# One decode step of an attention block: another order of the first loads, ScalarE sums 16 rows of query 0, one SBUF tensor for keys and values, other pieces for the last values

## The chip, the core and the metric

The kernel runs on one core of a Trainium2 chip. The metric is the device time of one launch in microseconds, the median of several runs. The engines that matter are VectorE (DVE), TensorE (PE), ScalarE (ACT), and the queue of SyncE (SP), which issues all but one of the loads. The loads run on 16 DMA engines.

## What is computed

A transformer block for one new token in each of two sequences: attention over a cache of 8192 positions with 16 heads of 256, and then a bilinear gated feed-forward layer. All is float32.

```
h  = x + (softmax(q k^T / 16) v) wo     q = layernorm(x) wq, B=2, H=16, Sk=8192, Dh=256, D=448
h2 = h + ((n wg) * (n wu)) wd           n = layernorm(h), F=1792
```

Each of the 32 pairs of head and sequence (called a query here, numbers 0 to 31) reads its own 8 MB of keys and 8 MB of values. With the weights that is 561 MB in all.

## The kernel before

A query's keys and values stand as 128 partitions of 64 rows of 256 numbers; a load of all 64 rows is 8192 KB. The scores are made on DVE: one TENSOR_TENSOR multiplies rows by the query's vector in place, one TENSOR_REDUCE sums each row. The product with the values is made on TensorE: for two rows at a time a matmul of 2 columns of `p` against 2x256 values, which the chip runs as two instructions, so that 64 rows are 64 rows of MATMUL in the trace.

Keys stand in a ring of 112 rows (`k_sb`). Even queries start at row 0 and odd ones at row 48, so that rows 48 to 63 are shared by neighbours. `score_parts` begins each query with those 16 shared rows: when the first product and sum are done, the shared rows are free and `load_k(n + 1)` can be issued. Values stand in `v_sb`, 64 rows; `load_v` of a query waits until TensorE has read the values of the query before.

Program order is set by the loop over `n` at the end of `decode_block`: load the values of query `n-1`, first scores of query `n` (with the softmax of query `n-1` between product and sum), load the keys of query `n+1`, further pieces of the values, the rest of the scores, the product with the values (`mix`), the maximum (`top`). SP takes its loads strictly in that order and waits in it; the DMA engines work off what SP has issued in order. Waits are worked out by a recorder (`Orders`) from the regions that each operation reads and writes.

The last queries are written apart: `LATE` gives the pieces in which their values are loaded and where, `FINE` makes queries 30 and 31 score 16 rows at a time, so that places come free earlier. Behind the last values come the feed-forward weights: gate (`wg`, one load), up (`wu`, two), down (`wd`, four). `open_sums` puts the sum so far (`h_sb`) into PSUM, `mixed` transposes the attention output, `project` is the gate or up product, `down` the down product. All lines of the trace read L229 or L176, since one helper writes all instructions and one issues all loads.

At the start the first weights (`d_w0`, 896 KB) are loaded, then query 0's keys in two pieces: rows 40 to 63, then rows 0 to 39. The product of the first piece goes into `v_sb`. TensorE makes the two heads' query vectors for both sequences before the loop.

Of the kernel before, what the change touches and what calls it, by code (L numbers as in the profile page):

```python
# [6 lines left out]
AF = mybir.ActivationFunctionType  # L7
# [11 lines left out]
OVER = HC  # L19

AHEAD = 24
FIRST = ((NJ - AHEAD, NJ), (0, NJ - AHEAD))


LATE = (
    ((48, None), (16, None)),
    ((32, None), (32, None)),
    ((32, None), (32, ("k", 0))),
    ((16, ("k", 32)), (32, ("v", 32)), (16, ("v", 0))),
)  # L30
WQ, WO = 3 * 2 * DH + DH, 2 * D
WALL = 2 * WQ + 4 * WO
# [183 lines left out]
def decode_block(nc, x, k_cache, v_cache, w, wg, wu, wd, out):  # L216
# [25 lines left out]
        put("PE", "transpose", out, in_, ident[:n, :n], r=(*r, "ident"), w=w, mark=mark)  # L242

    sb("align", P, ALIGN)
    k_sb = sb("k_sb", P, 2 * NJ - OVER, DH)
    v_sb = sb("v_sb", P, NJ, DH)
    w_sb = sb("w_sb", P, WALL)
    buffers = {"k": k_sb, "v": v_sb}
    v_flat = v_sb.rearrange("p j d -> p (j d)")

    def guest(name, at, rows, *shape):

        n = 1
        for k in shape:
            n *= k
        o.homes[name] = ("v", at, n)
        got = v_flat[:rows, at : at + n]
        if len(shape) > 1:
            dims = "abc"[: len(shape)]
            got = got.rearrange(f"p ({' '.join(dims)}) -> p {' '.join(dims)}", **dict(zip(dims, shape)))  # L260
        return got
# [5 lines left out]
        h, b = divmod(i, B)  # L267
        return cache[b, h].rearrange("(p j) d -> p j d", p=P)[:, lo:hi, :]

    def load_keys(name, cache, i, lo, hi, buf, at, event=None):  # L270
        o.load(
            "SP", name, buffers[buf][:, at : at + hi - lo, :], keys(cache, i, lo, hi),
            writes=[(buf, at * DH, (at + hi - lo) * DH)], event=event,
        )

    def k_base(i):
        return i % 2 * (NJ - OVER)

    def load_k(i, lo=0, hi=NJ):
        load_keys(f"d_k_{i}_{lo}", k_cache, i, lo, hi, "k", k_base(i) + lo)  # L280

    def v_parts(i):
        got, lo = [], 0
        for n, place in LATE[i - EARLY] if i >= EARLY else ((NJ, None),):
            buf, at = place or ("v", lo)
            got.append((lo, lo + n, buf, at))
            lo += n
        return got

    def load_v(i, part):  # L290
        lo, hi, buf, at = part
        load_keys(f"d_v_{i}_{lo}", v_cache, i, lo, hi, buf, at, "e_v" if i < LOOP else None)

    def load_w(name, k, lo, hi, event=None):
        o.load("SP", name, w_sb[:, lo:hi], w[k][:, lo:hi], writes=[("w", lo, hi)], event=event)
# [4 lines left out]
    def wo_at(h):  # L300
        return 2 * WQ + h % 4 * WO

    load_w("d_w0", 0, 0, WQ)
    for lo, hi in FIRST:
        load_k(0, lo, hi)

    ident = sb("ident", P, P)
    put("POOL", "memset", ident, 0.0, w=["ident"])
# [77 lines left out]
    def q_at(h):  # L386
        return h % 2 * (1 + h // 2 % 2)

    for k in range(2):
        for b in range(B):  # L390
            for c in range(DC):
                at = c * 2 * DH + (k * DH if c < DC - 1 else 0)
                mm(
                    q_ps[b][:, :DH], xb[:, c + (k if c == DC - 1 else 0), b, :],
                    w_sb[:, at : at + DH], c == 0, c == DC - 1, r=["xb", ("w", 0, WQ)],
                    w=[f"q_ps{b}"], mark="PE" if c == DC - 1 else None,
                )
# [6 lines left out]
    o.settle("PE", ["DVE", "POOL", "ACT"])
    mm(
        acc_ps, ident[:B, :B], x_sb[:, :D], True, False, r=["ident", "x_sb"], w=["acc_ps"],
        mark="PE",
    )
# [34 lines left out]
    def score_parts(i):  # L443
        if i == 0:
            return list(FIRST)
        at = [(k - 1) % (NJ // HC) * HC if i % 2 == 0 else k * HC for k in range(NJ // HC)]
        if i in FINE:
            return [(lo, lo + HC) for lo in at]
        return [(at[0], at[0] + HC), (at[1], at[1] + NJ - HC)]

    def scores(i, part, between=None):
        h, b = divmod(i, B)
        s, name = s_t[i % 2], f"s{i % 2}"
        lo, hi = score_parts(i)[part]
        at = k_base(i) + lo
        kt = k_sb[:, at : at + hi - lo, :]
        qk, there = kt, ("k", at * DH, (at + hi - lo) * DH)
        if i == 0 and part == 0:
            qk, there = v_sb[:, : hi - lo, :], ("v", 0, (hi - lo) * DH)
        q, slot = qs[b], q_at(h)  # L460
        here = ("k", at * DH, (at + hi - lo) * DH)
        dve(
            "tensor_mul", qk, kt, q[:, slot, :][:, None, :].to_broadcast([P, hi - lo, DH]),
            r=[here, (f"q{b}", slot, slot + 1)], w=[there],
        )
        if between is not None:
            between()
        dve("tensor_reduce", s[:, lo:hi], qk, axis=AX.X, op=ALU.add, r=[there], w=[(name, lo, hi)])

    def top(i):  # L470
        dve("tensor_reduce", m, s_t[i % 2], axis=AX.X, op=ALU.max, r=[f"s{i % 2}"], w=["m"],
# [24 lines left out]
    def mix(i, parts):  # L496
        k = other(i)
        with common(i):
            take("e_v", i, 16)
            for lo, hi, buf, at in parts:  # L500
                for t in range(lo // 2, hi // 2):
                    g, j = 32 * (t % 4), at + 2 * t - lo
                    mm(
                        o_ps[k][g : g + 2, :], p_t[k][:, 2 * t : 2 * t + 2],
                        buffers[buf][:, j : j + 2, :], t < 4, t >= NJ // 2 - 4,
                        r=[f"p{k}", (buf, j * DH, (j + 2) * DH)], w=[f"o_ps{k}"],
                        mark="PE" if t == hi // 2 - 1 else None,
                    )

# [71 lines left out]
    def group(t, q):  # L581
        return t[:, q * YW : (q + 1) * YW]

    late_at = [HC * DH]

    def late_guest(name, rows, *shape):
        got = guest(name, late_at[0], rows, *shape)
        late_at[0] += o.homes[name][2]
        assert late_at[0] <= 2 * HC * DH
        return got  # L590

    h_sb = late_guest("h_sb", B, DC * P)
# [19 lines left out]
    for n in range(NQ + 1):  # L612
        hp, at = divmod(n, 2 * B)
        parts = v_parts(n - 1) if n > 0 else []
        if n > 0:
            load_v(n - 1, parts[0])
        if n < NQ:
            scores(n, 0, (lambda: softmax(n - 1)) if n > 0 else None)
        else:
            softmax(n - 1)  # L620
        if late is not None:
            mix(n - 2, late)
            mixed(n - 2)
# [12 lines left out]
        if n == NQ:
            norm_last()
        else:
            for part in range(1, len(score_parts(n))):
                scores(n, part, norm_last if part == 1 else None)  # L640
        if n == NQ:
            mix(n - 1, parts[:-1])
            open_sums()
            mix(n - 1, parts[-1:])
            mixed(n - 1)
        elif n + 1 < NQ and len(parts) > 1:
            late = parts[1:]
            mix(n - 1, parts[:1])
        elif n > 0:
            mix(n - 1, parts)  # L650
            mixed(n - 1)
        if at == 2 and hp + 1 < H // 2:
            queries(n - 1, hp + 1)
        if n < NQ:
            if n == 0:
                o.ops["PE"].append(lambda: turns())
            top(n)

    k_flat = k_sb.rearrange("p j d -> p (j d)")
    places = {"wd": 0, "wg": (NJ - OVER) * DH, "wu": (NJ - OVER) * DH + NF * D}  # L660
    wd_t, wg_t, wu_t = (k_flat[:, places[n] :][:, : NF * D] for n in ("wd", "wg", "wu"))
    for name, t, src in (("wg", wg_t, wg), ("wu", wu_t, wu)):
        for k, half in enumerate(PIECES[name]):
            o.load("SP", f"d_{name}_{k}", t[:, half], src[:, half],
                   writes=[("k", places[name] + half.start, places[name] + half.stop)])
    at = 0
    for n in DOWN:
        o.load("SP", f"d_wd_{at}", wd_t[:, at * D : (at + n) * D], wd[:, at * D : (at + n) * D],
               writes=[("k", at * D, (at + n) * D)])
        at += n  # L670

    o.load(
# [6 lines left out]

    def project(out, out_name, t, name, k, between=None):  # L680
        wide, piece = WIDE[{"wg": "B_w_gate", "wu": "B_w_up"}[name]][k], PIECES[name][k]
        here = ("k", places[name] + piece.start, places[name] + piece.stop)
        t = t[:, piece]
        for c in range(DC):
            for g in range(4):
# [172 lines left out]
```

## Time and profile before

| | |
|---|---|
| time, median of 3 runs | 1301.44 us (1301.37 to 1301.44) |
| span of the profiled execution, first to last instruction | 1300.46 us (1300.5 on the page) |
| time less span: what lies around the span, as the profile has no time of its own | 0.98 us |
| DVE busy | 1130.8 us (87%) |
| PE busy (matmuls) | 488.8 us (38%) |
| ACT busy | 62.6 us (5%) |
| moved by DMA | 561.45 MB, mean 432 GB/s |
| mean granted TensorE clock, share of full speed | 0.654 |

Busy time of an engine counts only instructions that compute. The span is cut into 40 slices on the page, and each digit is the busy share in tenths. The granted clock of TensorE takes two levels, 0.5 and 1.0 of full speed.

### The profile page before, as it was taken

How to read it: one execution, taken by the hardware profiler on the slowest of the kernel's cores; microseconds unless marked ns; L12 is line 12 of the kernel's file. 1: busy time of each engine (PE TensorE's matmuls, PEld its weight loads, DVE VectorE, ACT ScalarE, POOL GpSimd, SP SyncE). 2: the span in 40 equal slices, each digit the busy share in tenths (PEclk: the TensorE clock that was granted, in tenths of full speed). 3: DMA queues.
4: the chain of work that ended last, by engine and by line, in shares of the span. 5: the costliest groups of instructions: out<-in, count | busy, mean ns of one | idle time of the engine just before them, and what ended most of it. 6: DMA issues, size and time to landing. Idle time of an engine off the chain costs nothing.

```text
span 1300.5 us, 6955 instructions
## 1 busy us (share of the span) xinstructions
PE 488.8 (38%) x2972; PEld 168.9 (13%) x2972; DVE 1130.8 (87%) x275; ACT 62.6 (5%) x184; POOL 1.4 (0%) x9
## 2 busy tenths in 40 slices
PE   3035422363331633215343063432424334243368
PEld 2011100120100201002101021010111001010113
DVE  7996988888988689888889868898888897889991
ACT  1000000000000000000000000000000000000000
POOL 0000000000000000000000000000000000000000
PEclk8566756686656766558666576665766667666578
DMA  9999999999999999999999999999999999999998
GB/s 414 423 434 448 424 437 431 427 441 423 448 424 435 448 423 443 427 439 429 435 435 423 433 448 423 448 424 443 427 443 427 423 436 445 426 438 429 435 433 374
DMA packets 12111, 561.45 MB, mean 432 GB/s; under 512 B 1602, under 2 KB 1732, under 8 KB 1988
## 3 DMA queue, kind: packets, MB, share of 16 engines
q1 hardware_dynamic: 12096, 561.30, 99.8%
q8 instruction: 6, 0.10, 0.0%
q14 instruction: 5, 0.04, 0.0%
q10 hardware_dynamic: 4, 0.00, 0.0%
HBM read 561.19 MB, written 0.11 MB: 432 GB/s over the span
## 4 chain that ended last, share of the span: by engine, by line
DMA 70%; DVE 29%; PE 0%; issue 0%; SPq 0%
DMA k_sb<-in_A_k_cache_dram 68%; DVE k_sb L229 14%; DVE s L229 14%; DMA k_sb<-in_wd_dram 2%; DVE nm L229 0%; PE y_ps L229 0%; SPq L176 0%; DVE m L229 0%; PE sm L229 0%; DVE v_sb L229 0%; DVE rl L229 0%
## 5 line engine op out<-in xcount | busy, mean ns | idle before, releaser
L229 DVE TENSOR_TENSOR k_sb<-k_sb,q 128x12288 f32<-128x12288 f32 (+2 forms) x67 | 549.6, 8203 | 130.3 <-DMA k_sb<-in_A_k_cache_dram 130.3
L229 DVE TENSOR_REDUCE s<-k_sb 128x48 f32<-128x12288 f32 (+2 forms) x67 | 549.3, 8198 | 0.2
L229 PE MATMUL o_ps<-v_sb,p 128*2 128x512 f32 x2000 | 288.2, 739 | 397.7 <-PEq L183 387.6
L229 PEld LDWEIGHTS o_ps<-v_sb,p 128*2 128x2 f32 x2000 | 53.7, 97 | 603.8 <-issue 591.3
L229 PE MATMUL sm<-nm,ones 1*128 1x1 f32 x64 | 16.6, 326 | 191.7 <-PEq L183 175.1
L229 PE MATMUL sm<-ident,m 128*1 128x128 f32 x32 | 10.9, 341 | 137.0 <-PEq L183 106.1
L229 PE MATMUL q_ps<-w_sb,xb 128*128 128x256 f32 (+1 forms) x172 | 59.3, 503 | 0.0
L229 ACT ACTIVATE o_sb<-o_ps 128x512 f32<-128x512 f32 x32 | 19.1, 597 | 703.9 <-PE o_ps L229 703.9
L229 PE MATMUL sm<-sel,o_sb 128*128 128x1 f32 x256 | 33.7, 253 | 25.8 <-PEq L183 22.9
L229 PE MATMUL acc_ps<-w_sb,oT 128*2 128x448 f32 x60 | 36.6, 749 | 15.9 <-PEq L183 11.0
L229 PEld LDWEIGHTS sm<-nm,ones 1*128 1x128 f32 x64 | 14.6, 283 | 201.2 <-issue 183.5
L229 PEld LDWEIGHTS sm<-sel,o_sb 128*128 128x128 f32 x256 | 31.8, 195 | 55.6 <-issue 48.2
L229 PEld LDWEIGHTS q_ps<-w_sb,xb 128*128 128x128 f32 x172 | 33.7, 200 | 30.0 <-issue 27.6
L229 PE MATMUL sm<-lsum,ones 128*128 128x1 f32 x64 | 17.5, 342 | 26.0 <-PEq L183 23.1
L229 ACT ACTIVATE nb<-sm 128x1 f32<-128x1 f32 x32 | 5.5, 171 | 395.7 <-PE sm L229 395.7
L229 PEld LDWEIGHTS sm<-ident,m 128*1 128x1 f32 x32 | 2.6, 81 | 149.8 <-issue 115.3
L229 PEld LDWEIGHTS sm<-lsum,ones 128*128 128x128 f32 x64 | 15.6, 303 | 28.0 <-issue 24.7
L229 ACT ACTIVATE q<-q_ps,rstd 128x512 f32<-128x512 f32 (+1 forms) x18 | 11.5, 640 | 71.9 <-PE q_ps L229 71.9
L229 PE MATMUL o_ps<-k_sb,p 128*2 128x512 f32 x48 | 9.3, 934 | 6.1 <-DMA k_sb<-in_A_v_cache_dram 6.1
L229 ACT ACTIVATE p<-s,nb 128x64 f32<-128x64 f32 x32 | 11.1, 347 | 1.0
L229 DVE TENSOR_TENSOR v_sb<-k_sb,q 128x6144 f32<-128x6144 f32 x1 | 6.6, 6557 | 4.8 <-DMA k_sb<-in_A_k_cache_dram 4.8
L229 PE MATMUL q_ps<-k_sb,xr 128*32 128x256 f32 (+3 forms) x96 | 10.0, 506 | 1.6 <-DMA k_sb<-in_B_w_gate_dram 1.6
(79 smaller groups left out, 85.1 us busy)
## 6 DMA issues: line engine op xcount, KB each, us to landing
v_sb<-in_A_v_cache_dram SPq DMA_DIRECT2D x4, 4096.0 KB, 30.5
w_sb<-in_w_dram SPq DMA_DIRECT2D x3, 3584.0 KB, 37.8
v_sb<-in_A_v_cache_dram SPq DMA_DIRECT2D x1, 6144.0 KB, 24.3
k_sb<-in_A_k_cache_dram SPq DMA_DIRECT2D x1, 5120.0 KB, 24.6
v_sb<-in_A_v_cache_dram SPq DMA_DIRECT2D x2, 2048.0 KB, 27.3
k_sb<-in_A_v_cache_dram SPq DMA_DIRECT2D x1, 4096.0 KB, 35.3
k_sb<-in_B_w_gate_dram SPq DMA_DIRECT2D x1, 3136.0 KB, 32.4
k_sb<-in_A_k_cache_dram SPq DMA_DIRECT2D x1, 3072.0 KB, 11.6
```

Source lines behind the costliest of these rows:

```text
L229: o.put(engine, lambda: f(*args, **kw), r, w, mark, event)
```

## The change

Six edits, in the order of the program:

1. SP's first load is query 0's keys, rows 0 to 23, into the place of the values; then `d_w0`; then rows 24 to 63 into the ring. Even and odd queries change places in the ring (even ones at 48), so that query 1's keys (rows 0 to 63) overlap nothing of query 0's.
2. Of the 24 rows of query 0's first piece ScalarE sums 16, one ACTIVATE with an accumulator for each row; DVE sums 8. Head 1's query vectors are made behind that in program order, and TensorE's wait for the other engines (`settle`) ahead of its loop moves behind them too.
3. `k_sb` and `v_sb` become one tensor `c_sb` of 176 rows: ring 0 to 111, values from 112.
4. Query 28 is an ordinary query: its values come in one load of 64 rows, and TensorE's loop covers it. Queries 29, 30 and 31 load in pieces of 32 and 32, of 64, of 44 and 20 rows.
5. The product of query 30's first 16 rows goes to rows 160 to 175, so that `load_k(31)` needs only the product and not the sum.
6. At the end `open_sums` stands before all of query 31's `mix`; the feed-forward weights take other places.

```diff
-FIRST = ((NJ - AHEAD, NJ), (0, NJ - AHEAD))
+FIRST = ((0, AHEAD), (AHEAD, NJ))
+RING = 2 * NJ - OVER
 LATE = (
-    ((48, None), (16, None)),
-    ((32, None), (32, None)),
-    ((32, None), (32, ("k", 0))),
-    ((16, ("k", 32)), (32, ("v", 32)), (16, ("v", 0))),
+    ((32, RING), (32, RING + 32)),
+    ((64, NJ),),
+    ((44, RING + HC), (20, NJ)),
 )
...
     def k_base(i):
-        return i % 2 * (NJ - OVER)
+        return (1 - i % 2) * (NJ - OVER)
...
+    load_keys("d_k_first", k_cache, 0, *FIRST[0], RING)
     load_w("d_w0", 0, 0, WQ)
-    for lo, hi in FIRST:
-        load_k(0, lo, hi)
+    load_k(0, *FIRST[1])
...
-        at = [(k - 1) % (NJ // HC) * HC if i % 2 == 0 else k * HC for k in range(NJ // HC)]
+        at = [(k - i % 2) % (NJ // HC) * HC for k in range(NJ // HC)]
...
+        at = RING if i == 0 and part == 0 else k_base(i) + lo
+        to = RING + NJ - HC if i == NQ - 2 and part == 0 else at
...
-        dve("tensor_reduce", s[:, lo:hi], qk, axis=AX.X, op=ALU.add, r=[there], w=[(name, lo, hi)])
+        if i == 0 and part == 0:
+            for j in range(HC):
+                row = ("c", (to + j) * DH, (to + j + 1) * DH)
+                act(t[:, j, :], t[:, j, :], AF.Copy, accum_out=s[:, lo + j : lo + j + 1],
+                    r=[row], w=[row, (name, lo + j, lo + j + 1)])
+            t, there, lo = t[:, HC:, :], ("c", (to + HC) * DH, (to + hi - lo) * DH), lo + HC
+        dve("tensor_reduce", s[:, lo:hi], t, axis=AX.X, op=ALU.add, r=[there], w=[(name, lo, hi)])
...
         if n < NQ:
+            if n == 0:
+                first_queries(0)
+                open_sum()
             scores(n, 0, (lambda: softmax(n - 1)) if n > 0 else None)
+            if n == 0:
+                first_queries(1)
+                o.settle("PE", ["DVE", "POOL", "ACT"])
...
         if n == NQ:
-            mix(n - 1, parts[:-1])
             open_sums()
-            mix(n - 1, parts[-1:])
+            mix(n - 1, parts)
             mixed(n - 1)
...
-    places = {"wd": 0, "wg": (NJ - OVER) * DH, "wu": (NJ - OVER) * DH + NF * D}
+    places = {"wg": 0, "wu": NF * D, "wd": (NJ + 20) * DH}
```

How SP's queue begins before the change (a row is a load, its shape in numbers per partition, and the engines that it waits for; 6144 numbers are 24 rows of keys, 16384 are 64):

```order
L176 DMA w_sb<-in_w_dram 128x1792 [waits barrier_Pool_Activation_PE_DVE_SP_release]
L176 DMA k_sb<-in_A_k_cache_dram 128x6144
L176 DMA k_sb<-in_A_k_cache_dram 128x10240
L176 DMA k_sb<-in_A_k_cache_dram 128x16384 [waits DVE]
L176 DMA v_sb<-in_A_v_cache_dram 128x16384 [waits DVE,PE]
```

And with the change:

```order
L176 DMA c_sb<-in_A_k_cache_dram 128x6144 [waits barrier_Pool_Activation_PE_DVE_SP_release]
L176 DMA w_sb<-in_w_dram 128x1792
L176 DMA c_sb<-in_A_k_cache_dram 128x10240
L176 DMA c_sb<-in_A_k_cache_dram 128x16384
L176 DMA c_sb<-in_A_v_cache_dram 128x16384 [waits PE,ACT,DVE]
```

Query 0's first keys stand ahead of the weights, query 1's keys (the fourth row) wait for nothing, and query 0's values wait for ScalarE as well.

Near the end of SP's queue before the change, from the values of query 27 to the first load of the gate weights:

```order
L176 DMA v_sb<-in_A_v_cache_dram 128x16384 [waits PE]
L176 DMA k_sb<-in_A_k_cache_dram 128x16384 [waits DVE]
L176 DMA v_sb<-in_A_v_cache_dram 128x12288 [waits PE]
L176 DMA k_sb<-in_A_k_cache_dram 128x16384 [waits DVE]
L176 DMA v_sb<-in_A_v_cache_dram 128x4096
L176 DMA v_sb<-in_A_v_cache_dram 128x8192 [waits PE]
L176 DMA k_sb<-in_A_k_cache_dram 128x16384 [waits DVE]
L176 DMA v_sb<-in_A_v_cache_dram 128x8192 [waits PE] x2
L176 DMA k_sb<-in_A_v_cache_dram 128x8192 [waits DVE]
L176 DMA k_sb<-in_A_v_cache_dram 128x4096 [waits DVE]
L176 DMA v_sb<-in_A_v_cache_dram 128x8192 [waits PE]
L176 DMA v_sb<-in_A_v_cache_dram 128x4096 [waits PE]
```

And with the change, from the same load on:

```order
L176 DMA c_sb<-in_A_v_cache_dram 128x16384 [waits PE]
L176 DMA c_sb<-in_A_k_cache_dram 128x16384 [waits DVE]
L176 DMA c_sb<-in_A_v_cache_dram 128x16384 [waits PE]
L176 DMA c_sb<-in_A_k_cache_dram 128x16384 [waits DVE]
L176 DMA c_sb<-in_A_v_cache_dram 128x8192 [waits PE]
L176 DMA c_sb<-in_A_k_cache_dram 128x16384 [waits DVE]
L176 DMA c_sb<-in_A_v_cache_dram 128x8192 [waits DVE]
L176 DMA c_sb<-in_A_v_cache_dram 128x16384 [waits DVE,PE]
L176 DMA c_sb<-in_A_v_cache_dram 128x11264 [waits PE]
L176 DMA c_sb<-in_A_v_cache_dram 128x5120 [waits PE]
```

Before, 48 rows of query 28's values stand ahead of query 30's keys (the fourth row) and 16 rows behind them; now all 64 stand ahead.

TensorE from query 31's maximum on, before (`o_ps` is the product with the values, `h_ps` in `o_ps` and `y_ps` with `pair` are `open_sums`):

```order
L229 MATMUL sm<-ident,m 1x128 [waits DVE]
L229 MATMUL sm<-nm,ones 128x1 [waits ACT,DVE]
L229 MATMUL sm<-lsum,ones 128x1 [waits ACT]
L229 MATMUL o_ps<-k_sb,p 2x512 [waits d_v_31_0]
L229 MATMUL o_ps<-k_sb,p 2x512 x7
L229 MATMUL o_ps<-v_sb,p 2x512 [waits d_v_31_16]
L229 MATMUL o_ps<-v_sb,p 2x512 x15
L229 MATMUL o_ps<-v_sb,ident 2x128 [waits DVE]
L229 MATMUL y_ps<-v_sb,pair 32x112 x4
L229 MATMUL o_ps<-v_sb,p 2x512 [waits d_v_31_48]
L229 MATMUL o_ps<-v_sb,p 2x512 x7
```

And with the change:

```order
L229 MATMUL sm<-ident,m 1x128 [waits DVE]
L229 MATMUL sm<-nm,ones 128x1 [waits ACT,DVE]
L229 MATMUL sm<-lsum,ones 128x1 [waits ACT]
L229 MATMUL o_ps<-c_sb,ident 2x128 [waits DVE]
L229 MATMUL o_ps<-c_sb,ident 2x128 x3
L229 MATMUL y_ps<-c_sb,pair 32x112 x4
L229 MATMUL o_ps<-c_sb,p 2x512 [waits d_v_31_0]
L229 MATMUL o_ps<-c_sb,p 2x512 x21
L229 MATMUL o_ps<-c_sb,p 2x512 [waits d_v_31_44]
L229 MATMUL o_ps<-c_sb,p 2x512 x9
```

The matmuls of `open_sums`, which wait for DVE's copies of `h_sb`, now stand ahead of all 32 of query 31's product, where before 24 of those stood ahead of them.

## Rows read from the trace of the kernel before

**Rows 1.** The page: busy share of the DMA engines in 40 slices.

```profile
DMA  9999999999999999999999999999999999999998
```

**Rows 2.** Chain that ended last, in order of time: start us, us, what.

```profile
1.64 24.58 DMA k_sb<-in_A_k_cache_dram
...
57.05 27.09 DMA k_sb<-in_A_k_cache_dram
...
93.13 38.10 DMA k_sb<-in_A_k_cache_dram
...
1091.11 29.66 DMA k_sb<-in_A_k_cache_dram
...
1129.76 29.64 DMA k_sb<-in_A_k_cache_dram
...
1159.42 4.43 DVE k_sb L229
...
1194.47 4.33 DVE k_sb L229
...
1266.00 30.43 DMA k_sb<-in_wd_dram
```

**Rows 3.** Timeline of the start: start us, us, engine, operation, count [idle before].

```profile
7.30 9.25 PE L229 MATMUL q_ps<-w_sb,xb 128*128 128x256 f32 x32
...
11.10 0.47 ACT L229 ACTIVATE q<-q_ps,rstd 128x256 f32<-128x256 f32 x1 [1.85 <-PE q_ps L229]
12.83 6.56 DVE L229 TENSOR_TENSOR v_sb<-k_sb,q 128x6144 f32<-128x6144 f32 x1 [4.83 <-DMA k_sb<-in_A_k_cache_dram]
...
19.42 6.55 DVE L229 TENSOR_REDUCE s<-v_sb 128x24 f32<-128x6144 f32 x1
...
26.24 10.82 DVE L229 TENSOR_TENSOR k_sb<-k_sb,q 128x10240 f32<-128x10240 f32 x1 [0.27 <-DMA k_sb<-in_A_k_cache_dram]
...
53.88 0.19 ACT L229 ACTIVATION_READ_ACCUMULATOR p<-s,nb 128x1 f32 x1
```

**Rows 4.** Timeline near the end: value products of queries 27 and 28, DVE in query 30.

```profile
1140.22 9.29 PE L229 MATMUL o_ps<-v_sb,p 128*2 128x512 f32 x64 [12.73 <-PEq L183]
...
1173.94 7.78 PE L229 MATMUL o_ps<-v_sb,p 128*2 128x512 f32 x48 [7.95 <-DMA v_sb<-in_A_v_cache_dram]
...
1225.25 4.42 DVE L229 TENSOR_REDUCE s<-k_sb 128x16 f32<-128x4096 f32 x1
```

**Rows 5.** Timeline of the tail: query 31's softmax and product, feed-forward layer.

```profile
1265.16 0.22 DVE L229 TENSOR_REDUCE m<-s 128x1 f32<-128x64 f32 x1
...
1268.20 0.72 DVE L229 COPY v_sb<-acc_ps 2x448 f32<-2x448 f32 x2
...
1271.23 3.61 PE L229 MATMUL o_ps<-v_sb,p 128*2 128x512 f32 x32
...
1274.77 0.40 PE L229 MATMUL o_ps<-v_sb,ident 2*2 2x128 f32 x8
...
1274.99 0.37 PE L229 MATMUL y_ps<-v_sb,pair 2*32 2x112 f32 x8
1275.63 1.90 PE L229 MATMUL o_ps<-v_sb,p 128*2 128x512 f32 x16 [0.27 <-DMA v_sb<-in_A_v_cache_dram]
...
1281.57 0.57 DVE L229 COPY xr<-sm 128x96 f32<-128x96 f32 x3 [0.74 <-PE sm L229]
...
1283.13 3.63 PE L229 MATMUL q_ps<-k_sb,xr 128*32 128x512 f32 x16 [1.60 <-DMA k_sb<-in_B_w_gate_dram]
...
1296.47 2.03 PE L229 MATMUL y_ps<-k_sb,v_sb 128*32 128x112 f32 x64 [0.71 <-DMA k_sb<-in_wd_dram]
1298.10 0.16 PEld L229 LDWEIGHTS y_ps<-k_sb,v_sb 128*32 128x32 f32 x8 [0.22 <-DMA k_sb<-in_wd_dram]
```

**Rows 6.** Windows of 1 us: busy (instructions) by engine, granted TensorE clock, DMA share, GB/s.

```profile
1283.00:1284.00 1.00, 0.87 (x8) 0.45 (x12) 0.29 (x2) 0.00 (x0) 0.00 (x0) 0.50 1.00 430
...
1288.00:1289.00 1.00, 1.00 (x18) 0.58 (x14) 0.00 (x0) 0.00 (x0) 0.00 (x0) 0.93 1.09 462
```

More of the change, by code (lines that the diff above doesn't have):

```diff
@@ L244, in decode_block @@
     sb("align", P, ALIGN)
-    k_sb = sb("k_sb", P, 2 * NJ - OVER, DH)
-    v_sb = sb("v_sb", P, NJ, DH)
+    c_sb = sb("c_sb", P, RING + NJ, DH)
+    v_sb = c_sb[:, RING:, :]
     w_sb = sb("w_sb", P, WALL)
-    buffers = {"k": k_sb, "v": v_sb}
-    v_flat = v_sb.rearrange("p j d -> p (j d)")
+    c_flat = c_sb.rearrange("p j d -> p (j d)")
     def guest(name, at, rows, *shape):
@@ L255, in guest @@
             n *= k
-        o.homes[name] = ("v", at, n)
-        got = v_flat[:rows, at : at + n]
+        at += RING * DH
+        o.homes[name] = ("c", at, n)
+        got = c_flat[:rows, at : at + n]
         if len(shape) > 1:
@@ L268, in keys, with rows, load_keys @@
         return cache[b, h].rearrange("(p j) d -> p j d", p=P)[:, lo:hi, :]
-    def load_keys(name, cache, i, lo, hi, buf, at, event=None):
+    def rows(at, n):
+        return ("c", at * DH, (at + n) * DH)
+    def load_keys(name, cache, i, lo, hi, at, event=None):
         o.load(
-            "SP", name, buffers[buf][:, at : at + hi - lo, :], keys(cache, i, lo, hi),
-            writes=[(buf, at * DH, (at + hi - lo) * DH)], event=event,
+            "SP", name, c_sb[:, at : at + hi - lo, :], keys(cache, i, lo, hi),
+            writes=[rows(at, hi - lo)], event=event,
         )
     def k_base(i):
-        return i % 2 * (NJ - OVER)
+        return (1 - i % 2) * (NJ - OVER)
     def load_k(i, lo=0, hi=NJ):
-        load_keys(f"d_k_{i}_{lo}", k_cache, i, lo, hi, "k", k_base(i) + lo)
+        load_keys(f"d_k_{i}_{lo}", k_cache, i, lo, hi, k_base(i) + lo)
     def v_parts(i):
         got, lo = [], 0
-        for n, place in LATE[i - EARLY] if i >= EARLY else ((NJ, None),):
-            buf, at = place or ("v", lo)
-            got.append((lo, lo + n, buf, at))
+        for n, at in LATE[i - EARLY] if i >= EARLY else ((NJ, RING),):
+            got.append((lo, lo + n, at))
             lo += n
@@ L290, in load_v @@
     def load_v(i, part):
-        lo, hi, buf, at = part
-        load_keys(f"d_v_{i}_{lo}", v_cache, i, lo, hi, buf, at, "e_v" if i < LOOP else None)
+        lo, hi, at = part
+        load_keys(f"d_v_{i}_{lo}", v_cache, i, lo, hi, at, "e_v" if i < LOOP else None)
     def load_w(name, k, lo, hi, event=None):
@@ L387, in q_at, with first_queries @@
         return h % 2 * (1 + h // 2 % 2)
-    for k in range(2):
+    def first_queries(k):
         for b in range(B):
@@ L402, in decode_block, with open_sum @@
             )
[L404 to L408, printed above, removed]
+    def open_sum():
+        mm(
+            acc_ps, ident[:B, :B], x_sb[:, :D], True, False, r=["ident", "x_sb"], w=["acc_ps"],
+            mark="PE",
+        )
     s_t = [sb(f"s{k}", P, NJ) for k in range(2)]
@@ L454, in scores @@
         lo, hi = score_parts(i)[part]
[L455 to L459, printed above, removed]
+        at = RING if i == 0 and part == 0 else k_base(i) + lo
+        to = RING + NJ - HC if i == NQ - 2 and part == 0 else at
+        k_t, t = (c_sb[:, r : r + hi - lo, :] for r in (at, to))
+        here, there = rows(at, hi - lo), rows(to, hi - lo)
         q, slot = qs[b], q_at(h)
-        here = ("k", at * DH, (at + hi - lo) * DH)
         dve(
-            "tensor_mul", qk, kt, q[:, slot, :][:, None, :].to_broadcast([P, hi - lo, DH]),
+            "tensor_mul", t, k_t, q[:, slot, :][:, None, :].to_broadcast([P, hi - lo, DH]),
             r=[here, (f"q{b}", slot, slot + 1)], w=[there],
@@ L499, in mix @@
             take("e_v", i, 16)
-            for lo, hi, buf, at in parts:
+            for lo, hi, at in parts:
                 for t in range(lo // 2, hi // 2):
@@ L504, in mix @@
                         o_ps[k][g : g + 2, :], p_t[k][:, 2 * t : 2 * t + 2],
-                        buffers[buf][:, j : j + 2, :], t < 4, t >= NJ // 2 - 4,
-                        r=[f"p{k}", (buf, j * DH, (j + 2) * DH)], w=[f"o_ps{k}"],
+                        c_sb[:, j : j + 2, :], t < 4, t >= NJ // 2 - 4,
+                        r=[f"p{k}", rows(j, 2)], w=[f"o_ps{k}"],
                         mark="PE" if t == hi // 2 - 1 else None,
@@ L582, in group @@
         return t[:, q * YW : (q + 1) * YW]
-    late_at = [HC * DH]
+    late_at = [0]
     def late_guest(name, rows, *shape):
@@ L588, in late_guest @@
         late_at[0] += o.homes[name][2]
-        assert late_at[0] <= 2 * HC * DH
+        assert late_at[0] <= HC * DH
         return got
@@ L657, in decode_block @@
             top(n)
-    k_flat = k_sb.rearrange("p j d -> p (j d)")
-    places = {"wd": 0, "wg": (NJ - OVER) * DH, "wu": (NJ - OVER) * DH + NF * D}
-    wd_t, wg_t, wu_t = (k_flat[:, places[n] :][:, : NF * D] for n in ("wd", "wg", "wu"))
+    places = {"wg": 0, "wu": NF * D, "wd": (NJ + 20) * DH}
+    wd_t, wg_t, wu_t = (c_flat[:, places[n] :][:, : NF * D] for n in ("wd", "wg", "wu"))
     for name, t, src in (("wg", wg_t, wg), ("wu", wu_t, wu)):
@@ L664, in decode_block @@
             o.load("SP", f"d_{name}_{k}", t[:, half], src[:, half],
-                   writes=[("k", places[name] + half.start, places[name] + half.stop)])
+                   writes=[("c", places[name] + half.start, places[name] + half.stop)])
     at = 0
@@ L668, in decode_block @@
         o.load("SP", f"d_wd_{at}", wd_t[:, at * D : (at + n) * D], wd[:, at * D : (at + n) * D],
-               writes=[("k", at * D, (at + n) * D)])
+               writes=[("c", places["wd"] + at * D, places["wd"] + (at + n) * D)])
         at += n
@@ L681, in project @@
         wide, piece = WIDE[{"wg": "B_w_gate", "wu": "B_w_up"}[name]][k], PIECES[name][k]
-        here = ("k", places[name] + piece.start, places[name] + piece.stop)
+        here = ("c", places[name] + piece.start, places[name] + piece.stop)
         t = t[:, piece]
@@ L759, in down @@
                     wd_t[:, k * D + q * YW : k * D + (q + 1) * YW], False, k == NF - 1,
-                    r=[f"hmT{n // 2}", ("k", k * D, (k + 1) * D)], w=["y_ps"],
+                    r=[f"hmT{n // 2}", ("c", places["wd"] + k * D, places["wd"] + (k + 1) * D)],
+                    w=["y_ps"],
                     mark="PE" if k == NF - 1 and q == YN - 1 else None,
```

## The prediction

> **What bounds the kernel now.** I read the page's slices first. The DMA engines are busy 90% or more in 39 of 40 slices [rows 1]: whatever the compute engines do, bytes arrive at one rate. The chain of waits, in order of time, says the same in another way: it goes from key load to key load. The keys of query 28 land at 1091.11 + 29.66 = 1120.77 and those of query 29 at 1129.76 + 29.64 = 1159.40 [rows 2], 38.63 us apart, for two loads of 8192 KB: 19.32 us each, 434 GB/s. DVE waits for each, though it is the busiest engine. In the early stretch with a weight load between, keys land at 57.05 + 27.09 = 84.14 and at 93.13 + 38.10 = 131.23 [rows 2]; the 47.09 us between are 8.46 us more for 3.67 MB, again 434 GB/s. So three loads cost what their bytes cost, and no fixed price per load can be seen.
>
> From 1159.42 on it is different. DVE has no row of waiting for keys between query 29's first product (1159.42) and query 30's first (1194.47) [rows 2]: it is the bound there. Query 30's keys had landed earlier. By the rate, 48 rows of query 28's values are 14.49 us behind 1159.4, at 1173.9, which is when TensorE starts on them (1173.94) [rows 4]; the keys follow 19.32 later, at 1193.3.
>
> The tail is bound by DMA again, narrowly. The up and down weights are in the queue by 1266.00 and the chain waits 30.43 us for a piece of the down weights [rows 2]. TensorE's slack on the way there is little. The normalised input `xr` is ready at 1281.57 + 0.57 = 1282.14, and the gate product starts at 1283.13, on the load: 0.99 us. Before the last 64 down matmuls TensorE stands 0.71 us for a load, and in them 0.22 us for the last one [rows 5]. Sum: 1.9 us. If the tail's compute comes later by less, nothing changes; the rest goes to the end in full.
>
> **The start.** The first bytes still move at 1.64, and there is no gap to take away behind them, so the three reordered loads give nothing by themselves. Query 0's first keys and `d_w0` both land at about 12.8, as the same bytes landed before (DVE started at 12.83 on them). TensorE then needs what it needed before, 11.10 - 7.30 = 3.8 us to the first query vector, and ScalarE 0.47: DVE's product starts at 17.1 instead of 12.83, 4.3 later [rows 3]. It ends at 23.7 (6.56). DVE sums 8 rows of 24, 6.55/3 = 2.2, and is done at 25.9. The next piece lands at 26.2 as before, since the bytes ahead are the same. So the 4.3 us lost in front are given back by the 4.4 that DVE doesn't sum.
>
> ScalarE's 16 sums: no such row exists. An ACTIVATE of 256 numbers takes 0.47 and an accumulator read 0.19 [rows 3]; at most their sum, 0.66, each; at least 0.47: 7.5 to 10.6 us, so done at 31.2 to 34.3, and query 0's values are issued 5 to 8 us later than their former place behind 25.97 (19.42 + 6.55). It is covered: with query 1's keys issued at once, 17.7 MB are queued from 1.64, work until 42.5. If that cover is gone (over 1.0 us a row), DMA starves. Query 2's keys are issued by DVE at 57.05 while 26.1 MB last until 61.8: 4.7 us of room, against which DVE's start may slip by some tenths. Value: 0. A gain is bounded by the 1.64 us ahead of the first bytes, which no edit touches, and I allow 0.2 for the order of the first loads; a loss by about 1.
>
> **The middle.** One tensor and swapped halves of the ring leave every wait of queries 1 to 27 as it is: first part, then next keys. 0.
>
> **The end.** Here is the term. Query 28's 64 rows of values now all stand ahead of query 30's keys, which land at 1159.4 + 2 x 19.32 = 1198.1. DVE is ready at 1194.47, so it waits 3.6 us. Everything that DVE does behind it moves by that: query 31's maximum from 1265.16 [rows 5] to 1268.8. The saved wait of `load_k(31)` (it needs the product only, 4.4 us sooner) gives DVE nothing, since those keys land at 1198.1 + 9.7 (32 rows of values) + 19.3 = 1227.1, ahead of their use at about 1233.
>
> Does DMA starve? Query 30's values are one load and wait for DVE's last sum of query 30, 1225.25 + 4.42 = 1229.67 [rows 4], now 1233.3. What is queued ends with query 29's second half at 1227.1 + 9.7 = 1236.8: 3.5 us of room. They land at 1256.1, TensorE needs 9.3 (as in the loop [rows 4]), and the last 20 rows of query 31's values are issued at 1265.5; the 44 ahead of them last until 1256.1 + 13.3 = 1269.4. 4 us of room. So DMA ends as before, and the last values land at 1275.4 as before (TensorE started on them at 1275.63 [rows 5]).
>
> But TensorE is later. The copies of `h_sb` end at 1268.92 + 3.6 = 1272.5 [rows 5]. `open_sums` took 0.6 us (1274.77 to 1275.36) at the high clock; I take 1.1 at the low one: 1273.6. Then 64 instructions of query 31's product. Before, 48 of them were done before the last values came, and only 16 (1.90 us) were left: end at 1277.53. Now all 64 lie behind 1273.6. Bounds: 7.2 us at the high clock (3.61 for 32), 9.29 for a pass that begins at the low one [rows 4, 5]. I take the middle, 8.25: end at 1281.85, 4.3 later. Less 1.9 of slack: 2.4.
>
> The gate product begins after a pause at the low clock. Before, it ran at half clock from 1283.13 until about 1288.1, 5.0 us [rows 6]. The pass of 9.29 lost 2.1 us against 7.2, so some 4.1 at half speed. With 4.1 for the gate the change gives 0.45 back. The Trainium skill ("TensorE: Matmul & The Clock Gate", Part 1) says that sustained activity releases the clock and that the point of the rise isn't tied to the kernel's start. By it this term may differ from run to run, and no run here shows whether it does; the sum goes by the rows.
>
> Three loads fewer among the last values: 0 by the rate above. The Trainium skill ("DMA: Bandwidth & Descriptors", Anatomy of one DMA) gives each DMA of another kind of queue a fixed cost of about 2 us. By that three fewer would give 6 us, 1295.4; the weight load's 8.46 us for 3.67 MB shows none of it where loads queue up.
>
> **Sum.** Span 1300.46 + 2.4 - 0.45 = 1302.4; with the 0.98 around the span, 1303.4, against a median of 1301.44. That is +0.15%, within the 0.2% (2.6 us) that I take as what a measurement of this kernel can tell from no change.
>
> **Rivals.** *Slower by more than 0.2%*: TensorE's clock. Query 31's product runs as slowly as the loop's pass, and the gate product as before: end at 1273.6 + 9.29 = 1282.9, 5.4 later, less 1.9: +3.4, 1304.9. It decides from 8.6 us upward if the gate gives nothing back, 9.1 if it gives 0.45. For it: TensorE pauses between query 30's product and query 31's, as it did before. Against: `open_sums` already works at the low clock ahead of it. Chance 0.28, with ScalarE over 1.0 us a row counted in it at 0.03.
>
> *Hidden*: the clock is high during the product and rises sooner at the gate (half as long at the low clock, 2.5 us instead of 5.0, 1.2 back): 1273.6 + 7.2 = 1280.8, 3.3 later, less 1.9 and 1.2: 0.2. Or DVE's wait isn't 3.6. Then DMA ends it as before: 1301.2 (with the 0.2 of the start) to 1302.0. Chance 0.17.
>
> *Faster*: a fixed price per load or a shorter start that the trace hides. Against it: DMA at 9 from the first slice [rows 1]; even the whole 1.64 us ahead of the first bytes is less than 2.6. Chance 0.02. By the Trainium skill's figure above it would be 1295.4.
>
> **The numbers.** Forecast 0.53, from 1302.0 to 1304.0, value 1303.4. Faster 0.02; same 0.53 + 0.17 = 0.70; slower 0.28. The range takes the bounds of the end term, from DMA's own end (1301.2) to 1304.9.
>
> **What would show it.** Right: DVE idle about 3.6 us for query 30's keys near 1198; query 31's maximum near 1268.8; no wait for the gate or down weights in TensorE's rows; query 31's product ending near 1281 to 1283; DMA at 9 throughout, and its last load no later than 1298.3. Early: DVE's second product at 26.2 to 27, 16 ACTIVATE with accumulators ending before 35. Wrong if query 30's keys land by 1195, if values of query 30 or 31 are issued after the queue has run dry, or if the tail still waits for the down weights.

## The result and the profile after

Ten runs of the changed kernel have a median of 1304.66 us (1303.26 to 1306.64), against 1301.44 us before: ratio 1.0024 [1.0016, 1.0032]. The forecast of 1303.4 is 1.3 us short. The kernel is slower, by an amount on the border of the prediction's 0.2%; the price is that of the slower rival (1304.9), and the forecast's own band, 1302.0 to 1304.0, misses it. The ten fall into groups: four at 1303.3 to 1303.6, one at 1304.0, five at 1305.3 or more. The profiled execution (1305.79 us) is of the upper group. In nine runs the time is 1.28 to 1.36 us above the span of the same run; the highest, 1306.64, has a span of 1304.2 like the others of its group, and 1.1 us of it lie outside the span.

The page: span, and the slices of the DMA engines.

```profile
span 1304.5 us, 7000 instructions
...
DMA  9999999999999999999999999999999999999998
```

The slices are those of before [rows 1]: 4 us in 1300 don't show in tenths. The timeline of the start:

```profile
16.77 6.56 DVE L229 TENSOR_TENSOR c_sb<-c_sb,q 128x6144 f32<-128x6144 f32 x1 [8.78 <-ACT q L229]
...
23.37 2.29 DVE L229 TENSOR_REDUCE s<-c_sb 128x8 f32<-128x2048 f32 x1
23.69 0.18 ACT L229 ACTIVATION_READ_ACCUMULATOR c_sb<-c_sb 128x1 f32 x1
23.78 0.40 ACT L229 ACTIVATE c_sb<-c_sb 128x256 f32<-128x256 f32 x1
...
25.57 10.82 DVE L229 TENSOR_TENSOR c_sb<-c_sb,q 128x10240 f32<-128x10240 f32 x1
...
29.95 0.33 SPq L176 DMA_DIRECT2D c_sb<-in_A_v_cache_dram  x1
```

DVE's first product starts 3.9 us later than before (12.83 in [rows 3]), its sum is 4.3 us shorter, and the second product starts 0.7 us sooner than before (26.24). Its keys had landed by 25.57; the prediction had them at 26.2. ScalarE's sums end just ahead of 29.95, when query 0's values are issued and the queue still has work. The chain that ended last, in order of time (start us, us, what):

```profile
1159.52 4.43 DVE c_sb L229
...
1168.49 29.64 DMA c_sb<-in_A_k_cache_dram
1198.23 4.42 DVE c_sb L229
...
1269.02 0.23 DVE m L229
...
1272.15 0.65 DVE c_sb L229 x2
1272.84 0.60 PE o_ps L229 x8
1273.44 0.37 PE y_ps L229 x8
1273.82 9.68 PE o_ps L229 x64
1283.52 0.61 ACT o_sb L229
```

Query 29's first product starts at 1159.52, against 1159.42 [rows 2]: until there nothing is won or lost. Then a wait for keys stands where there was none, and behind 1198.23 no piece is a DMA any more; before, the chain ended on the down weights [rows 2]. The late keys, the late maximum and the 64 instructions of query 31's product are the new path. The timeline of the same places, with the issue of the last 20 rows of query 31's values and of the gate weights behind them:

```profile
1198.23 4.42 DVE L229 TENSOR_TENSOR c_sb<-c_sb,q 128x4096 f32<-128x4096 f32 x1 [3.66 <-DMA c_sb<-in_A_k_cache_dram]
...
1266.20 0.33 SPq L176 DMA_DIRECT2D c_sb<-in_A_v_cache_dram  x1
1266.57 0.43 SPq L176 DMA_DIRECT2D c_sb<-in_B_w_gate_dram  x1
...
1273.75 9.70 PE L229 MATMUL o_ps<-c_sb,p 128*2 128x512 f32 x64
...
1288.58 3.63 PE L229 MATMUL q_ps<-c_sb,xr 128*32 128x512 f32 x16 [0.67 <-DVE xr L229]
```

Windows of 1 us (busy time and instructions of each engine, granted TensorE clock, DMA share, GB/s), in query 31's product and in the gate product:

```profile
1278.00:1279.00 1.00, 1.00 (x12) 0.27 (x8) 0.00 (x0) 0.00 (x0) 0.00 (x0) 0.50 1.05 452
1279.00:1280.00 1.00, 1.00 (x16) 0.19 (x8) 0.00 (x0) 0.00 (x0) 0.00 (x0) 0.93 0.93 401
...
1286.00:1287.00 1.00, 0.40 (x9) 0.11 (x1) 0.46 (x2) 0.27 (x1) 0.00 (x0) 0.50 0.99 419
...
1292.00:1293.00 1.00, 1.00 (x8) 0.69 (x10) 0.20 (x2) 0.00 (x0) 0.00 (x0) 0.61 0.99 421
```

The product runs at a granted 0.50 (1.2 GHz) until about 1279.1, so for its first 5.4 us; from 1286.0 to about 1292.8 the clock is low again.

### The profile page after: what moved, and what is told of

The parts are those of the page before. It is cut to its first block, busy times and chain, and to the rows that moved or that the text cites. A ratio compares the mean times of both kernels' runs of the same rounds, so it can differ in the third digit from the quotient of the medians.

```text
span 1304.5 us, 7000 instructions
## 1 busy us (share of the span) xinstructions
PE 482.4 (37%) x2972; PEld 168.8 (13%) x2972; DVE 1126.7 (86%) x275; ACT 68.9 (5%) x216; POOL 1.4 (0%) x9
## 5 line engine op out<-in xcount | busy, mean ns | idle before, releaser
L229 DVE TENSOR_TENSOR c_sb<-c_sb,q 128x4096 f32<-128x4096 f32 (+1 forms) x68 | 556.1, 8178 | 142.4 <-DMA c_sb<-in_A_k_cache_dram 133.6
L229 DVE TENSOR_REDUCE s<-c_sb 128x16 f32<-128x4096 f32 (+1 forms) x68 | 551.6, 8111 | 0.2
L229 PE MATMUL o_ps<-c_sb,p 128*2 128x512 f32 x2048 | 293.3, 736 | 407.5 <-PEq L183 399.6
L229 PEld LDWEIGHTS o_ps<-c_sb,p 128*2 128x2 f32 x2048 | 54.9, 97 | 619.5 <-issue 610.0
L229 PE MATMUL acc_ps<-w_sb,oT 128*2 128x448 f32 x60 | 33.7, 696 | 15.8 <-PEq L183 11.0
L229 PE MATMUL sm<-lsum,ones 128*128 128x1 f32 x64 | 17.3, 340 | 26.2 <-PEq L183 24.0
L229 ACT ACTIVATE oT<-sm,rl 128x2 f32<-128x2 f32 x32 | 8.4, 262 | 38.4 <-PE sm L229 38.4
L229 PE MATMUL q_ps<-c_sb,xr 128*32 128x256 f32 (+3 forms) x96 | 9.5, 487 | 0.7 <-DVE xr L229 0.7
```

The costliest lines, as they stand in the source:

```text
L229: o.put(engine, lambda: f(*args, **kw), r, w, mark, event)
```

## The experiments

In what was expected, theory A is the prediction's end term taken at its measured size: query 30's keys come 3.6 us late, query 31's product with them, and TensorE's low clock decides what that costs. The rivals are told where they stand. Medians, beside those of the kernel before on the same chip (the intervals are some 1.2 us to either side, so that gains under 1 us are not clear of them):

| run | median us (lowest to highest) | before | ratio |
|---|---|---|---|
| e1_sums_between | 1304.11 (1303.15 to 1306.04) | 1301.54 | 1.0021 [1.0012, 1.0030] |
| e2_v28_split | 1302.48 (1301.31 to 1303.99) | 1301.54 | 1.0006 [0.9997, 1.0015] |
| e3_both | 1302.08 (1301.35 to 1303.17) | 1301.54 | 1.0005 [0.9996, 1.0014] |
| e4_before_v28_whole | 1304.75 (1304.36 to 1305.62) | 1301.54 | 1.0026 [1.0016, 1.0037] |
| e5_start_alone | 1301.60 (1301.31 to 1301.75) | 1301.42 | 1.0001 [0.9992, 1.0010] |
| e6_busy_product | 1303.62 (1302.68 to 1305.72) | 1301.42 | 1.0020 [1.0011, 1.0029] |
| e7_busy_both | 1302.86 (1302.18 to 1304.58) | 1301.42 | 1.0012 [1.0003, 1.0021] |
| e8_v28_whole_free_rows | 1302.22 (1301.34 to 1304.34) | 1301.46 | 1.0008 [0.9999, 1.0017] |

**The order at the end undone** (`open_sums` again between the pieces of the product):

```diff
         if n == NQ:
+            mix(n - 1, parts[:-1])
             open_sums()
-            mix(n - 1, parts)
+            mix(n - 1, parts[-1:])
```

> The changed kernel (1304.7 us) with open_sums back between the two pieces of query 31's product. Theory A (DVE's wait of 3.7 us for query 30's keys sets the size, the order of open_sums adds to it): query 31's product starts about 1.9 us sooner (near 1271.9 instead of 1273.8), the maximum of query 31 stays near 1269.0, 1302.5 to 1303.5. Rival B (the order of open_sums alone makes the loss): 1301.4 to 1301.8. Rival C (only the low clock of TensorE counts, wherever the product starts): no change, 1304 to 1305.

TensorE's timeline:

```profile
1271.12 8.08 PE L229 MATMUL o_ps<-c_sb,p 128*2 128x512 f32 x44
...
1279.65 2.74 PE L229 MATMUL o_ps<-c_sb,p 128*2 128x512 f32 x20
...
1287.00 3.56 PE L229 MATMUL q_ps<-c_sb,xr 128*32 128x512 f32 x16 [0.66 <-DVE xr L229]
```

The product starts 2.6 us sooner and ends 1.1 sooner (1282.39 against 1283.45): the 44 instructions take 8.08 us. The median gains 0.6 us, less than expected and not clear of the spread. In this profile the matmuls moved ahead run at the low clock (it rises near 1276.7 here) and shorten the path by 1.1 us only. The order is at most a small part.

**Query 28's values split again** (48 rows ahead of query 30's keys, 16 behind):

```diff
 LATE = (
+    ((48, RING), (16, RING + 48)),
...
-        to = RING + NJ - HC if i == NQ - 2 and part == 0 else at
+        to = at
```

> The changed kernel with query 28's values again in 48 and 16 rows, the 16 behind query 30's keys, and query 30's first product in place again (the free rows are then not free). Theory A: DVE no longer waits for query 30's keys, query 31's maximum is at 1265.2 to 1265.5, the product starts near 1270 and mostly fits into the slack of 1.9 us: 1301.4 to 1302.5. Rival B: the loss stays, 1304 or more. The keys of query 31 are issued 4.4 us later behind their product; if that matters, DMA shows a gap near 1203 and the time goes over 1303.

DVE waits for no keys. The median falls by 2.2 us, the most of any undoing, to 0.9 over before. What is left comes by another way: TensorE's timeline has query 30's product in one piece of 64 rows, and behind it the transpose of query 31's maximum.

```profile
1255.95 9.40 PE L230 MATMUL o_ps<-c_sb,p 128*2 128x512 f32 x64 [10.14 <-DMA c_sb<-in_A_v_cache_dram]
...
1266.99 0.27 PE L230 MATMUL sm<-ident,m 128*1 128x128 f32 x1
...
1297.87 2.06 PE L230 MATMUL y_ps<-c_sb 128*32 128x112 f32 x64 [0.70 <-DMA c_sb<-in_wd_dram]
```

The end waits for the down weights again, but these come 1.4 us later than before (1296.47 in [rows 5]). The profiled execution (1303.22) is the second slowest of the eleven, so the usual run loses less than 1.4.

**Both undone** (the two diffs above together):

> Both edits of the two runs before together. Theory A: 1301.2 to 1301.7, with all runs within 0.3 us of each other, since the tail is bound by DMA again. Rival (the 44 and 20 rows, or the one load of query 30's values, cost by themselves): over 1302.5.

1302.08, 0.5 over before: between the theory's figures and the rival's, so neither names all of it, and the runs spread over 1.8 us, not 0.3. Timeline of TensorE and a window of 8 us:

```profile
1269.56 8.00 PE L230 MATMUL o_ps<-c_sb,p 128*2 128x512 f32 x44
...
1297.88 2.00 PE L230 MATMUL y_ps<-c_sb 128*32 128x112 f32 x64 [0.71 <-DMA c_sb<-in_wd_dram]
```

```profile
1264.00:1272.00 8.00, 6.17 (x41) 2.36 (x37) 2.66 (x9) 1.47 (x5) 0.00 (x0) 0.76 0.83 329
```

DMA's share is 0.83 of these 8 us, 1.4 us of idle time, as much as the down weights are late in this execution, the slowest of the eleven (1303.17). Before it was 0.99 (422 GB/s) there. The last 20 rows of query 31's values are issued at 1265.72, behind the product of 64 rows, and the gate weights behind them at 1266.09 (1250.64 before): the prediction's "4 us of room" did not hold the rate here.

**Query 28's values whole, in the kernel before**:

```diff
 LATE = (
-    ((48, None), (16, None)),
```

> The kernel before with one edit alone: query 28's values in one load of 64 rows, so an ordinary query. Theory A: DVE waits some 3.7 us for query 30's keys near 1198, query 31's maximum comes near 1268.9, the end 1.5 to 3 us later: 1303 to 1304.5, and runs differ by 1 us or more. Rival B: no change, 1301.4.

1304.75, a little over what was expected. Here DVE waits 3.6 us too, but a second thing goes wrong, so the run doesn't price the wait. SP's timeline and a window:

```profile
1206.63 0.33 SPq L175 DMA_DIRECT2D k_sb<-in_A_k_cache_dram  x1
```

```profile
1205.00:1210.00 5.00, 2.65 (x16) 0.53 (x20) 5.00 (x2) 0.00 (x0) 0.00 (x0) 0.50 0.67 236
```

Query 31's keys wait for the sum of query 30's first rows, which is late as well; DMA falls to 236 GB/s, a third of 5 us is lost. So the free rows for query 30's product, which the prediction counted as giving nothing, are what keeps the whole load of query 28 from costing DMA time.

**The whole load with the free rows, nothing else** (the kernel before with the last diff and this):

```diff
         if i == 0 and part == 0:
             qk, there = v_sb[:, : hi - lo, :], ("v", 0, (hi - lo) * DH)
+        if i == NQ - 2 and part == 0:
+            qk, there = v_sb[:, NJ - HC :, :], ("v", (NJ - HC) * DH, NJ * DH)
```

> The kernel before with two edits: query 28's values in one load, and query 30's first product in free rows of the values, so that query 31's keys don't wait for the sum (in the run with the first edit alone they came late and DMA stood still for some 2 us near 1205). Theory A: no DMA gap there, DVE still waits 3.6 us for query 30's keys, and the tail's compute is late: 1302.5 to 1304.5. Rival F (in that run the gap in DMA was the loss, and DVE's wait costs nothing): 1301.4 to 1301.8.

1302.22, 2.5 below e4. Its windows and TensorE's timeline:

```profile
1205.00:1210.00 5.00, 2.36 (x12) 0.40 (x16) 5.00 (x2) 0.00 (x0) 0.00 (x0) 0.50 1.03 446
```

```profile
1274.68 3.61 PE L228 MATMUL o_ps<-v_sb,p 128*2 128x512 f32 x32
...
1278.73 1.90 PE L228 MATMUL o_ps<-v_sb,p 128*2 128x512 f32 x16
...
1285.27 3.25 PE L228 MATMUL q_ps<-k_sb,xr 128*32 128x512 f32 x16 [0.67 <-DVE xr L228]
```

DMA keeps its rate, and DVE's wait of 3.6 us stands alone. The product ends 3.1 us later than before; the slack of 1.9 and a gate product with less low clock (3.25 against 3.63) take the most of that: this execution took 1301.67, 0.2 over before, and 0.8 reaches the median. Theory A expected more; the figures of the rival fit only the lower runs (five of eleven are at or under 1301.8).

**The start alone** (the changed kernel with the tail's loads, order and places as before):

```diff
 LATE = (
+    ((48, RING), (16, RING + 48)),
     ((32, RING), (32, RING + 32)),
-    ((64, NJ),),
-    ((44, RING + HC), (20, NJ)),
+    ((32, RING), (32, NJ)),
+    ((16, NJ + 32), (32, RING + 32), (16, RING)),
 )
```

> The changed kernel's start (order of the first loads, ScalarE's 16 sums, one tensor, swapped halves of the ring) with the last queries as before the change (nine loads in the same sizes and the mirrored places, open_sums between, query 30's product in place). Theory A (the start is worth nothing): 1301.2 to 1301.6, DMA without a gap. Rival D (the start costs or gives something that the tail hid): outside 1301.0 to 1302.0.

1301.60 against 1301.42: the start, the one tensor and ScalarE's sums are worth nothing that shows, as predicted.

**TensorE kept busy ahead of the product** (six matmuls whose result nobody reads, before query 31's maximum and between its softmax matmuls):

```diff
+    def busy(n):
+        for _ in range(n):
+            mm(q_ps[1], ident, w_sb[:, :512], True, True, r=["ident", ("w", 0, 512)], w=["q_ps1"])
```

> The changed kernel with six matmuls of 512 columns added that nobody reads, on TensorE in its pauses between query 30's product and open_sums of query 31, so that it goes on working. Theory A with the clock: granted clock 1.0 through query 31's product, which takes 7.2 us instead of 9.7; 1302 to 1303, and the runs lie closer together. Rival E (the clock isn't what makes the product long, its matmuls are): no change, 1304 to 1306.

TensorE's timeline, and a window in the product:

```profile
1274.18 7.05 PE L229 MATMUL o_ps<-c_sb,p 128*2 128x512 f32 x64
...
1286.25 3.63 PE L229 MATMUL q_ps<-c_sb,xr 128*32 128x512 f32 x16 [0.67 <-DVE xr L229]
```

```profile
1276.00:1277.00 1.00, 1.00 (x16) 0.22 (x9) 0.00 (x0) 0.00 (x0) 0.00 (x0) 1.00 0.93 401
```

The same 64 instructions take 7.05 us instead of 9.70 at a granted 1.00: the size of the product is the clock's, shown directly. The product starts 0.4 us later behind the added matmuls. The median gains only 1.0 us, 1303.62 is 0.6 over the upper end of what was expected, and the runs spread as before. In this profile the gate product behind it is at the low clock again.

**The same to the end of the normalisation** (four more such matmuls, behind the product and in the normalisation):

```diff
+            busy(1)
             open_sums()
...
+    busy(1)
...
+    busy(2)
```

> The run before with four more such matmuls between query 31's product and the gate product. Theory A with the clock: the gate product too runs at clock 1.0 (the first 16 in 2.4 us instead of 3.6), the tail is bound by DMA again or nearly: 1301.4 to 1302.2. If the added matmuls delay the chain themselves: no better than the run before, or up to 1 us worse.

TensorE's timeline and a window in the gate product:

```profile
1286.32 1.91 PE L229 MATMUL q_ps<-c_sb,xr 128*32 128x512 f32 x16
...
1297.27 2.04 PE L229 MATMUL y_ps<-c_sb 128*32 128x112 f32 x64 [0.90 <-DMA c_sb<-in_wd_dram]
```

```profile
1287.00:1288.00 1.00, 1.00 (x12) 0.23 (x4) 0.00 (x0) 0.00 (x0) 0.00 (x0) 1.00 1.09 462
```

In this profile TensorE has the high clock through query 31's product and the gate product, and then the down weights end the kernel again, 0.8 us later than before. The lowest run, 1302.18, is 0.8 over before. The median gives back 1.8 of the 3.2 us lost, and this profile's late weights hold 0.8 that no clock gives back.

**The changed kernel again, three single executions** (no edit):

> The changed kernel as it is, for another profile beside its time. If TensorE's clock makes the spread from 1303.3 to 1306.6: a run under 1304 shows query 31's product in 8.5 us or less or the gate product at the low clock for under 4 us, a run over 1305 shows 9 us or more and over 4 us; DVE's wait for query 30's keys and its maximum near 1269 are the same in all.

> As the run before, once more: the end of query 31's product and the stretch at the low clock behind it account for the difference in time to the other profiles within 0.5 us.

> As the run before, once more: the same account within 0.5 us.

They took 1305.74, 1303.13 and 1303.04 us. TensorE's timeline in each, in this order:

```profile
1274.01 9.60 PE L229 MATMUL o_ps<-c_sb,p 128*2 128x512 f32 x64
```

```profile
1273.23 8.74 PE L229 MATMUL o_ps<-c_sb,p 128*2 128x512 f32 x64
...
1286.61 3.35 PE L229 MATMUL q_ps<-c_sb,xr 128*32 128x512 f32 x16 [0.67 <-DVE xr L229]
```

```profile
1273.28 8.37 PE L229 MATMUL o_ps<-c_sb,p 128*2 128x512 f32 x64
...
1286.29 3.56 PE L229 MATMUL q_ps<-c_sb,xr 128*32 128x512 f32 x16 [0.67 <-DVE xr L229]
```

And a window of the third:

```profile
1276.00:1277.00 1.00, 1.00 (x16) 0.19 (x8) 0.00 (x0) 0.00 (x0) 0.00 (x0) 1.00 0.93 401
```

DVE's wait is the same in all, and the maximum of query 31 comes at 1269.29, 1268.76 and 1268.66. The clock rises near 1279.2 in the first, 1276.7 in the second, 1276.0 in the third, and is low again ahead of and in the gate product for 6.8, 3.4 and 3.4 us. Stage by stage, in us:

| execution | product starts | product | its end to gate | gate to end | span |
|---|---|---|---|---|---|
| profiled above, 1305.79 | 1273.75 | 9.70 | 5.13 | 15.88 | 1304.46 |
| first, 1305.74 | 1274.01 | 9.60 | 5.23 | 15.57 | 1304.41 |
| second, 1303.13 | 1273.23 | 8.74 | 4.64 | 15.19 | 1301.80 |
| third, 1303.04 | 1273.28 | 8.37 | 4.64 | 15.43 | 1301.72 |

The last two are 2.66 and 2.74 us shorter than the profiled execution. 2.1 to 2.3 of that lie behind the start of the product, in the stages whose length follows the clock; 0.5 stand already at its start, of which 0.3 to 0.4 are DVE's earlier maximum. So most of the spread is the clock, and not all. In the third TensorE's weight load stands 0.21 us for the last down weights, until 1299.29: this execution of the lower group ends on DMA again, and with the high clock throughout e7's median, 1302.86, is only 0.2 us lower.

## Why the prediction was right and wrong

**Right.** The bound and its slack, and all the steps up to TensorE: keys at 1198.2 (1198.1 predicted), DVE's wait 3.66 (3.6), maximum 1269.02 (1268.8), product starting at 1273.75 (1273.6), gate at low clock for 4.2 us (4.1), start worth nothing (e5), ScalarE's sums done before 35. Three of its signs did not come: DVE's second product at 25.57 (26.2 to 27), query 31's product ending at 1283.45 (1281 to 1283), and the last load, told below. That 1304.66 lies under 1304.9 is partly luck, since the median falls into the gap between two groups of runs.

**The step that failed: the size of query 31's product.** "I take the middle, 8.25." It measured 9.70, 9.60, 8.74 and 8.37 in four executions: twice above the upper bound of 9.29, by 0.4 and 0.3, and never at or below the middle. The bounds were a pass at the high clock and one pass of the loop. That the first can happen is shown by e6 (7.05), but there TensorE worked up to the product. In the changed kernel it pauses on the way (small matmuls between waits for DVE and ScalarE), the clock stays at 0.50 for the first 2.7 to 5.4 us, and the pass is then one like the loop's. And the loop's passes are not all 9.29. In the kernel before, the 28 that stand as one row of 64 take 8.37 to 10.01 us, 9.15 on average; the shortest and the longest:

```profile
824.75 10.01 PE L229 MATMUL o_ps<-v_sb,p 128*2 128x512 f32 x64 [12.74 <-PEq L183]
...
940.69 8.37 PE L229 MATMUL o_ps<-v_sb,p 128*2 128x512 f32 x64 [12.91 <-PEq L183]
```

All four measured passes lie in that range. With 9.15 in place of 8.25 the prediction's own sum is 1304.3. The argument against the rival, that `open_sums` already works ahead of it, was worth nothing: a microsecond of small matmuls did not bring the rise. The points from which the rival decides were worked out wrongly too: 1277.53 - 1273.6 + 1.9 + 2.6 is 8.4 where it says 8.6, and 8.9 with the gate's 0.45 where it says 9.1, so the rival was nearer than it looked.

In the profiled execution the sum goes: span 1304.46 against 1302.4, 2.06 more. The product gives 1.45 of it (9.70 - 8.25) and its start 0.15. The stretch from its end to the gate gives 0.52: 5.13 us (1283.45 to 1288.58) against 1282.14 - 1277.53 = 4.61 before, since part of its small matmuls ran at the low clock, which the prediction had not counted. From the gate to the end it took 15.88 us where 15.94 was predicted.

**The run itself differs.** The sentence from the Trainium skill ("TensorE: Matmul & The Clock Gate", Part 1) that the point of the rise may differ from run to run, which no run showed then, is borne out: 1276.0 to 1279.2 in four executions of one program. The forecast's case is what the lower group does (1303.0 to 1304.0, with e9 seven of thirteen runs), the rival's what the upper one does (1305.3 and more, six of thirteen), and the median falls between. A single predicted value couldn't hold both; the error was to give the upper group 0.28, and to end the range at 1304.9.

**A smaller one: the 0.98 around the span.** It set the profiled span of before against the median. In single runs of the kernel before the time is 1.28 to 1.46 us above the span of the same run (1.33 in the profiled execution of the changed kernel), so the profiled execution of before was itself about 0.35 us above the median.

**Another, hidden in the result: "DMA ends as before", and three loads fewer at 0.** In the profile after, TensorE is the later one and no wait shows it, but the last down weights land late there too: issued at 1271.58 and 27.5 us on the way, so at 1299.1, against 1298.1 before (1266.95 and 31.1) and "no later than 1298.3" in the prediction. Where the compute is early enough TensorE waits for them, until 1297.27 (e7), 1297.87 (e2) and 1297.88 (e3), against 1296.47. In the runs that keep the old pieces of queries 30 and 31 the last weights land at 1297.9 (e5) and 1298.0 (e8). So the new pieces make them late. The "3.5 us" and "4 us of room" were counted from bytes issued and not yet landed; with so little ahead of it the queue still lost time, shown for e3 in 1264 to 1272. Whether the loads' sizes do it, or the gate weights that now wait behind query 30's product (issued at 1266.57, before at 1250.64), was not tried apart and stays open.

**The parts don't add up.** Undoing query 28's split gives 2.2 us, the order 0.6, both 2.6; put into the kernel before, the whole load with the free rows costs 0.8. What is missing there is in the pieces of queries 30 and 31. e1 and e8 both have the late keys and the order of before; they differ in those pieces, in where the weights go, and in the start, which e5 prices at nothing. e1 stands 2.6 over the kernel before and e8 0.8, and nine of e8's eleven runs are below the lowest of e1. In their profiles the stretch of query 31's product takes 11.27 us (1271.12 to 1282.39) and 9.00 (1271.63 to 1280.63), with the clock rising near 1276.7 and 1274.4. With the keys on time the same pieces cost about 0.4 (e3 against e5), which isn't clear of noise. How the pieces move the rise is not shown, and no run undoes them alone. That lateness within the slack of 1.9 us is free and pays in full behind it fits these figures, but is argued.

The cause in short: query 28's values in one load put 16 more rows ahead of query 30's keys and made DVE 3.6 us late, ahead of a tail with 1.9 us of slack (undone, 2.2 of 3.2 us come back); the new pieces of queries 30 and 31 make that lateness dearer; and TensorE's clock decides, run by run, over most of another 2.7 us.

## What to carry to other kernels

In a queue that is served in order, merging loads is judged by whose data stands behind the bytes that move ahead, not by the price of a load: here 16 rows ahead of one key load cost 3.6 us of DVE's time, and three loads fewer gave nothing back. Where lateness puts a block of matmuls behind a pause of TensorE, price it at the range of the passes that the trace already has, not at one of them, and count the small matmuls around it at the low clock too, and expect the kernel's time to split into groups. And "so many us still queued" is not the same as a queue that keeps its rate.

## What the runs showed of the hardware

- The granted clock rose at points 3.2 us apart (1276.0 to 1279.2) in four executions of the same program, in which query 31's maximum on DVE lay within 0.7 us. Most of the 2.7 us between their spans goes with it.
- The 64 instructions of a value product took from 7.05 (at a granted 1.00 throughout, e6) to 10.01 us (in the kernel before). The two levels of the clock are a factor of two, so even the slowest had part of its time at the high one.
- ScalarE's sums of 256 numbers come 0.40 us apart, less than an ACTIVATE of the query vectors' row (0.47) in [rows 3]. The accumulator read (0.18 to 0.19) adds nothing to that: it overlaps the end of its own ACTIVATE and the start of the next (23.69 to 23.87, with the next at 23.78). So the lower bound of the prediction was still too high.
